# Retention attention with two FFN layers on one core: late token differences formed wide, another pair order in the opening step, splits two groups ahead

## The chip, the cores and the metric

One core of a Trainium2 chip runs the whole program. The metric is device microseconds of one execution, as the median of the runs. PE is TensorE (matmuls), DVE VectorE, ACT ScalarE, POOL GpSimd, and SP the engine from whose queue nearly all DMAs are issued. Each engine works through its own queue in order, and engines wait for each other by semaphores.

## What is computed

```python
for t in range(S):                                   # B=2, H=8, S=768, D=64
    state = gamma * state + k[:, :, t] (outer) v[:, :, t]
    y[:, :, t] = scale * q[:, :, t] @ state
x = y.transpose(0, 2, 1, 3).reshape(1536, 512)
h = x @ w_in; x = (h / (1 + exp(-h))) @ w_out        # 512 -> 2048 -> 512
h = x @ w_in; out = max(0.01 * h, h) @ w_out         # second layer, other weights
```

The state decays per head with `gamma = 1 - 2^(-5-h)`. Both layers see 1536 tokens; their weights come to the kernel as int64 words, from which float values are decoded on the chip.

## The kernel before

**Precision.** Every float operand of a large matmul is split in a rounded part h and a remainder l (`halves`: a copy on ACT, L172, and a subtraction on DVE, L173), and a product is the sum of three matmuls (`TERMS`).

**Attention.** Twelve chunks of 128 tokens, one iteration j each. In program order an iteration holds: the scaled queries of chunk j+1 (POOL, L213), the scores of j+1 (PE, L235), the scaled keys of j (POOL, L218), the decayed state (POOL, L225), the values of j (PE, L255, L264, L272), the masked scores of j+1 (DVE), `store_x(j)`, which puts the outputs of chunk j where the FFN wants them, the new state, and what the dict `behind` names for this j. From chunk 5 on the queries stand on POOL.

**Tokens.** They are kept as four sets of 384, in two pairs p, called lanes a and b. `put_first` stores the first set of a pair (`xf`, and its halves in `xa`). `put_second` forms for the second set differences `tm` on DVE (L302, L303), its halves in `xb`, and on POOL (L305, L306) two more differences in place of `xf`, chunk by chunk (128 x 256 elements each). `split_t(p, n)` makes the halves of `tm` (n = 0) and of the differences in `xf` (n = 1) into `T4[p]`, 128 x 1536 at once.

**Weights.** A weight block is loaded by two DMAs of 512 KB on SP (`load_w`, L119) into one of two staging buffers, then converted in pieces: `words` (ACT, L125 and L127), `clamp` (DVE, L131 and L135), `sign` (DVE, L142; it gives the staging buffer back, and `signed` issues the next load behind it), `low` (DVE, L149). A converted block goes to DRAM (`keep_w`, SP, L154), or is split at once (`direct`). For an up block POOL also forms four sums (`sums`, L169) into `sf`, and `split_a`, `split_s` split the blocks and the sums.

**Up projection.** Per layer eight steps; a step computes with block k a 2 x 2 arrangement of (output halves) x (sets) by seven products instead of eight. A product is 12 matmuls of 384 columns, six per lane (L357). Product 1, then 6, 7 and 4, add up in a PSUM pair X (two alternate between steps); product 2 goes to a pair Z; 5, then 3, to a pair V. After 1, 6 and 7 ACT copies X (L386) to `ct[0]`, `ct[1]`, `ct[2]`; after 2, 7 and 3 DVE adds a copy to Z or V (L390), and ACT applies the activation (L399 or L401). `keep` writes a step's result g, 1.5 MB, to DRAM (SP, L406); it stands in the step behind. `begin` writes the first step, lane by lane; `rest` each other step, in the order 6, 5, 2, 7, 1 (of the next step), 4, 3, with conversion pieces between products from `up_tasks`.

**Down projection.** 24 groups n: three token sets s of 512 and eight blocks i, 24 matmuls of 512 columns each (L434). For a group a block of g is fetched from DRAM (`fetch_g`, SP, L422) and split (`split_g`, gh). Weights of the first blocks are split before; in groups with s = 0 the remaining six are fetched from DRAM (L159) and split into `wt`. Layer 0's down projection also converts the eight up blocks of layer 1: `todo` has 32 pieces, spread over 22 groups. `finish_x` writes the end of a token set through `put_first` and `put_second` for the next layer.

**What sets the order.** All is written by hand under a manual schedule: the order in the code is the order in each engine's queue. SP's queue is shared by loads, keeps and fetches; a load that waits for `sign` holds up the fetches behind it.

Of the kernel before, what the change touches and what calls it, by code (L numbers as in the profile page):

```python
# [41 lines left out]
def retention_moe_kernel(ctx: ExitStack, tc: tile.TileContext, att, w1, w2, cst, out):  # L42
# [121 lines left out]
    def sums(w):  # L164
        A21, A22, A11, A12 = (blocks(w)[:, n] for n in range(4))
        S1, S2, S3, S4 = (sf[:, n] for n in range(4))
        for o, a, b, op in ((S1, A21, A22, ALU.add), (S3, A11, A21, ALU.subtract),
                            (S2, S1, A11, ALU.subtract), (S4, A12, S2, ALU.subtract)):
            nc.gpsimd.tensor_tensor(out=o, in0=a, in1=b, op=op)  # L169
# [118 lines left out]
    def put_first(s, a, b, ys, kept=False):  # L288
# [3 lines left out]
        for i, y in enumerate(ys):  # L292
            if not kept:
                nc.scalar.activation(out=f[:, i], in_=y, func=AF.Copy)
        for i, y in enumerate(ys):
            halves(h[:, i], l[:, i], y)

    def put_second(s, a, b, ys):
# [5 lines left out]
        halves(h, l, ys[1])  # L304
        nc.gpsimd.tensor_tensor(out=f[:, 0], in0=t[:, 1], in1=f[:, 0], op=ALU.subtract)  # L305
# [149 lines left out]
    with tc.manual_schedule():  # L455
# [32 lines left out]
        second_w = [[(l, 1, (i + 2) % Q) for i in range(Q)] for l in range(2)]  # L488
# [19 lines left out]
        def pieces(w, end=keep_w):  # L508
# [6 lines left out]
            8: lambda: (low(wa), sums(wa), split_t(0, 0)), 9: lambda: (split_a(wa), split_t(0, 1)),  # L515
            10: lambda: (split_s(wa), words(wb)),
# [27 lines left out]
        def up_tasks(layer, k):  # L544
            t = [[] for _ in range(7)]
            if layer == 0:
                if k == 0:
                    wd = first_w[3]
                    return [[lambda: split_t(1, 0)], [lambda: clamp(wb)], [lambda: signed(wb)],
                            [lambda: (low(wb), sums(wb)), lambda: split_t(1, 1)],  # L550
                            [lambda: split_a(wb)], [lambda: split_s(wb), lambda: words(wc)],
                            [lambda: clamp(wc)], [lambda: signed(wc)]]
                if k == 1:
                    wd = first_w[3]
                    return [[lambda: (low(wc), sums(wc))], [lambda: words(wd)],
                            [lambda: split_a(wc)], [lambda: split_s(wc)], [lambda: clamp(wd)],
                            [lambda: signed(wd)], [lambda: (low(wd), sums(wd))]]
                if k + 1 < Q:
                    a = first_w[k + 1]
                    t[0].append(lambda: split_a(a))  # L560
                    t[1].append(lambda: split_s(a))
# [216 lines left out]
```

## Time and profile before

| what | value |
|---|---|
| median of the runs (three) | 649.32 us (645.4 to 650.17) |
| the profiled execution's own time | 649.08 us |
| its span, first to last instruction | 647.3 us |
| PE busy | 577.3 us, 89% |
| DVE, ACT, POOL busy | 341.7, 284.9, 110.1 us |
| mean granted clock of PE | 0.944 of full speed |

A busy share counts time in which an engine executes. What an engine waits for is in the list of its waits, and a timeline row carries in brackets how long the engine was idle ahead of it and what released it. The granted clock is the share of full speed that PE had in a stretch.

### The profile page before, as it was taken

How to read it: one execution, taken by the hardware profiler on the slowest of the kernel's cores; microseconds unless marked ns; L12 is line 12 of the kernel's file. 1: busy time of each engine (PE TensorE's matmuls, PEld its weight loads, DVE VectorE, ACT ScalarE, POOL GpSimd, SP SyncE). 2: the span in 40 equal slices, each digit the busy share in tenths (PEclk: the TensorE clock that was granted, in tenths of full speed). 3: DMA queues.
4: the chain of work that ended last, by engine and by line, in shares of the span. 5: the costliest groups of instructions: out<-in, count | busy, mean ns of one | idle time of the engine just before them, and what ended most of it. 6: DMA issues, size and time to landing. Idle time of an engine off the chain costs nothing.

```text
span 647.3 us, 7975 instructions
## 1 busy us (share of the span) xinstructions
PE 577.3 (89%) x3222; PEld 510.3 (79%) x3222; DVE 341.7 (53%) x359; ACT 284.9 (44%) x337; POOL 110.1 (17%) x112
## 2 busy tenths in 40 slices
PE   9647488998888869989999979999999899999996
PEld 7546378998888857767878868999999688888885
DVE  5436364676778667546454756565665571320410
ACT  2012134666666565345324425656665470321401
POOL 3353613132333000000010242222220000000000
PEclk9768678998999979999999988999999899999999
DMA  8656001456777887664656620877773690540701
GB/s 334 256 160 231 1 2 65 164 192 230 260 261 270 287 281 267 231 229 162 218 199 184 216 89 4 274 258 244 257 271 121 224 363 31 196 129 12 249 1 65
DMA packets 35705, 121.19 MB, mean 187 GB/s; under 512 B 3282, under 2 KB 3410, under 8 KB 33620
## 3 DMA queue, kind: packets, MB, share of 16 engines
q1 hardware_dynamic: 35376, 120.34, 54.0%
q8 instruction: 25, 0.41, 0.3%
q10 hardware_dynamic: 292, 0.34, 0.2%
q14 instruction: 12, 0.10, 0.0%
HBM read 81.87 MB, written 38.80 MB: 186 GB/s over the span
## 4 chain that ended last, share of the span: by engine, by line
PE 60%; DVE 16%; DMA 8%; ACT 7%; issue 5%; POOL 3%; SPq 1%; ACTq 0%; DVEq 0%; POOLq 0%
PE p L357 27%; PE p L434 27%; DMA c<-g 4%; DVE r L142 3%; DVE r L149 3%; DVE w L173 2%; ACT w L172 2%; PE p L235 2%; PE p L255 2%; POOL sf L169 1%; PE p L264 1%; DMA sf<-g 1%; ACT c L386 1%; DMA r<-scr 1%; DVE big L390 1%
## 5 line engine op out<-in xcount | busy, mean ns | idle before, releaser
L357 PE MATMUL p<-tt,w 128*128 128x384 f32 x768 | 149.6, 346 | 18.7 <-ACT c L386 9.9
L357 PEld LDWEIGHTS p<-tt,w 128*128 128x128 f32 x768 | 138.9, 194 | 22.9 <-ACT c L386 12.2
L173 DVE TENSOR_TENSOR w<-c,w 128x1024 fp32r<-128x1024 f32 x46 | 56.6, 1230 | 122.3 <-ACT w L172 121.9
L434 PE MATMUL p<-w,wt 128*128 128x512 f32 x432 | 100.0, 391 | 4.7 <-ACT w L172 2.4
L434 PE MATMUL p<-wt,w 128*128 128x512 f32 x432 | 99.1, 390 | 1.4 <-ACT big L452 1.4
L434 PEld LDWEIGHTS p<-w,wt 128*128 128x128 f32 x432 | 80.9, 188 | 23.4 <-ACT w L172 3.6
L434 PEld LDWEIGHTS p<-wt,w 128*128 128x128 f32 x432 | 80.8, 188 | 19.1 <-ACT big L452 2.2
L172 ACT ACTIVATE w<-c 128x1024 fp32r<-128x1024 f32 x46 | 48.9, 1063 | 83.8 <-DMA c<-g 66.9
L434 PE MATMUL p<-w,w 128*128 128x512 f32 x288 | 71.8, 407 | 10.8 <-ACT w L172 7.7
L357 PE MATMUL p<-xa,w 128*128 128x384 f32 x384 | 76.9, 350 | 1.2 <-ACT c L386 1.2
L434 PEld LDWEIGHTS p<-w,w 128*128 128x128 f32 x288 | 56.3, 197 | 25.5 <-ACT w L172 9.3
L386 ACT ACTIVATE c<-p 128x768 f32<-128x768 f32 (+1 forms) x54 | 39.8, 741 | 81.1 <-PE p L357 70.3
L357 PEld LDWEIGHTS p<-xa,w 128*128 128x128 f32 x384 | 71.1, 198 | 2.5 <-ACT c L386 2.2
L390 DVE TENSOR_TENSOR big<-p,c 128x768 f32<-128x768 f32 (+1 forms) x54 | 46.7, 866 | 41.9 <-PE p L357 24.3
L169 POOL TENSOR_TENSOR sf<-r 128x256 f32<-128x256 f32 x32 | 36.6, 1164 | 173.4 <-DVE r L149 83.4
L149 DVE CUSTOM_DVE_ANT_0 r<-r,u 128x2048 uint16<-128x2048 uint16 x32 | 42.0, 1314 | 1.2
L127 ACT ACTIVATE u<-ws 128x1024 int32<-128x1024 uint32 x32 | 36.2, 1133 | 12.2 <-DVE r L149 12.2
L142 DVE SCALAR_TENSOR_TENSOR r<-ws,r 128x1024 int32<-128x1024 int32 x32 | 41.3, 1289 | 0.4
L125 ACT ACTIVATE r<-ws 128x1024 f32<-128x1024 f32 x32 | 36.3, 1135 | 9.8 <-DMA scr<-r 9.8
L305 POOL TENSOR_TENSOR big<-big 128x256 f32<-128x256 f32 (+2 forms) x9 | 8.3, 925 | 180.4 <-DMA ws<-w_dram 90.1
L173 DVE TENSOR_TENSOR w<-sf,w 128x1024 fp32r<-128x1024 f32 x18 | 22.0, 1223 | 32.2 <-ACT w L172 32.2
L357 PE MATMUL p<-xb,w 128*128 128x384 f32 x192 | 36.5, 337 | 0.7 <-DVE big L390 0.7
(74 smaller groups left out, 497.7 us busy)
## 6 DMA issues: line engine op xcount, KB each, us to landing
ws<-w_dram SPq DMA_DIRECT2D x64, 512.0 KB, 5.1
g<-big SPq DMA_DIRECT2D x16, 1536.0 KB, 6.2
c<-g SPq DMA_DIRECT2D x46, 512.0 KB, 5.5
scr<-r SPq DMA_DIRECT2D x20, 512.0 KB, 6.0
r<-scr SPq DMA_DIRECT2D x20, 512.0 KB, 7.1
att_a<-att_dram SPq DMA_DIRECT2D x18, 512.0 KB, 6.1
att_b<-att_dram SPq DMA_DIRECT2D x6, 512.0 KB, 8.4
out_dram<-big SPq DMA_DIRECT2D x11, 256.0 KB, 2.1
```

What stands on the lines that cost most here:

```text
L125: nc.scalar.activation(out=r.bitcast(F32), in_=t[:, :, :, 1].bitcast(F32), func=AF.Abs)
L127: nc.scalar.activation(out=u, in_=t[:, :, :, 0].bitcast(U32), func=AF.Copy, scale=2.0 ** -29)
L142: nc.vector.scalar_tensor_tensor(out=r, in0=t[:, :, :, 1], scalar=-0x40000000, in1=r, op0=ALU.bitwise_and, op1=ALU.bitwise_or)
L149: nc.vector.tensor_tensor(out=r, in0=r, in1=u, op=ALU.add)
L169: nc.gpsimd.tensor_tensor(out=o, in0=a, in1=b, op=op)
L172: nc.scalar.activation(out=h, in_=s, func=AF.Copy)
L173: nc.vector.tensor_tensor(out=l, in0=s, in1=h.bitcast(F32), op=ALU.subtract)
L235: nc.tensor.matmul(out=sc[:, r, c], lhsT=kT[s, c], rhs=q[s, c], start=True, stop=True)
L357: nc.tensor.matmul(out=o, lhsT=a[:, ta, k * 128:k * 128 + 128], rhs=rhs(p, tb, k), start=(begin and m == 0), stop=(end and m == 5), skip_g ...
L386: nc.scalar.activation(out=ct[n][:, c, 0:N], in_=self.X[:, c, 0:N], func=AF.Copy)
L390: nc.vector.tensor_tensor(out=self.block(f, half, lanes), in0=t[:, c, 0:N], in1=ct[n][:, c, 0:N], op=ALU.add)
L434: nc.tensor.matmul(out=y, lhsT=l, rhs=r, start=(i == 0 and f == 0 and n == 0), stop=(i == Q - 1 and f == 1 and n == 2),)
```

## The change

It is several edits of the hand-written order:

1. `put_second` no longer has the two POOL subtractions. `rest_t(p)` does them once per pair, 128 x 768 elements each: in attention at j = 10 and j = 11, behind POOL's last queries, and at layer 0's end behind `finish_x`. The sums of the first weight block are divided over j = 8, 9 and 10, its `split_s` moves to j = 11 and `split_t(0, 1)` into the opening step. `put_first` splits before it copies.
2. `begin` puts half products of the two lanes in another order: 1a 2a 1b 6a 2b 5a 7a 5b 6b 4a 3a 7b, then product 1 of the next step by lanes, 4b, 3b.
3. `rest` has the order 6, 2, 5, 7, 1, 4, 3, and the keep of the step before stands behind product 2.
4. The conversion pieces stand at other products. Steps 6 and 7 convert one weight block instead of two; down blocks 6 and 7 of layer 0 join layer 1's up blocks in `todo`, which now has 40 pieces, over 21 groups.
5. In the down projection the split of a block of g stands two groups ahead (one before), its fetch three (two before), and the first two splits stand in the last up step.

The diff, cut to its core:

```diff
-        nc.gpsimd.tensor_tensor(out=f[:, 0], in0=t[:, 1], in1=f[:, 0], op=ALU.subtract)
+    def rest_t(p):
+        f, t = xf[p], tm[p]
         nc.gpsimd.tensor_tensor(out=f[:, 0], in0=t[:, 1], in1=f[:, 0], op=ALU.subtract)
         nc.gpsimd.tensor_tensor(out=f[:, 1], in0=f[:, 1], in1=t[:, 1], op=ALU.subtract)
...
-            8: lambda: (low(wa), sums(wa), split_t(0, 0)), 9: lambda: (split_a(wa), split_t(0, 1)),
-            10: lambda: (split_s(wa), words(wb)),
+            8: lambda: (low(wa), sums(wa, (0,)), split_t(0, 0)), 9: lambda: (sums(wa, (1,)), split_a(wa)),
+            10: lambda: (sums(wa, (2, 3)), rest_t(0), words(wb)), 11: lambda: (split_s(wa), rest_t(1)),
...
-                (6, a, lambda l: s.copy(1, l)), (1, b, lambda l: s.copy(0, l)),
-                (7, a, lambda l: s.copy(2, l)), (2, b, lambda l: s.add(0, 0, 0, s.Z, l)),
+                (1, b, lambda l: s.copy(0, l)), (6, a, lambda l: s.copy(1, l)),
+                (2, b, lambda l: s.add(0, 0, 0, s.Z, l)), (5, a, lambda l: None),
...
-            seq = (6, 5, 2, 7, 1, 4, 3) if n else (6, 5, 7, 2, 4, 3)
+            seq = (6, 2, 5, 7, 1, 4, 3) if n else (6, 2, 5, 7, 0, 4, 3)
...
                     tasks[2].append(lambda: fetch_g(layer, 0, 0))
-                    tasks[5] += [lambda: split_g(layer, 0, 0), lambda: fetch_g(layer, 0, 1)]
-                    tasks[6] += [lambda: fetch_w(second_w[layer][0])]
+                    tasks[4] += [lambda: fetch_g(layer, 0, 1), lambda: split_g(layer, 0, 0)]
+                    tasks[5] += [lambda: fetch_w(second_w[layer][0])]
+                    tasks[6] += [lambda: split_g(layer, 0, 1)]
...
             steps[Q - 1].keep()
+            fetch_g(layer, 0, 2)
...
-            todo = [p for w in first_w[Q:] for p in pieces(w)] if layer == 0 else []
+            if layer == 0:
+                for w in second_w[0][6:] + first_w[Q:]:
+                    todo += pieces(w, third if w[1] else keep_w)
...
                 if n + 2 < SETS * Q:
-                    fetch_g(layer, *divmod(n + 2, Q))
-                if n + 1 < SETS * Q:
-                    split_g(layer, *divmod(n + 1, Q))
+                    split_g(layer, *divmod(n + 2, Q))
+                if n + 3 < SETS * Q:
+                    fetch_g(layer, *divmod(n + 3, Q))
...
-                    for t in todo[n * len(todo) // 22:(n + 1) * len(todo) // 22]:
+                for t in todo[n * len(todo) // 21:(n + 1) * len(todo) // 21]:
```

POOL's queue in attention, from the sums of the first weight block on: L213 are queries, L218 keys, L225 the state's decay, L169 sums (`sf`), L305 to L308 the token differences (`big`).

```order
+L169 TENSOR_TENSOR sf<-r_74 128x256
 L213 TENSOR_TENSOR att_a<-att_a,gst 128x512
 L218 TENSOR_TENSOR att_a<-att_a,cs 128x512
 L225 TENSOR_TENSOR gst<-gst,cs 128x256
-L305 TENSOR_TENSOR big<-big 128x2x128
-L306 TENSOR_TENSOR big<-big 128x2x128
+L169 TENSOR_TENSOR sf<-r_74 128x256
 L213 TENSOR_TENSOR att_b<-att_b,gst 128x512
```

The narrow pair ahead of the last queries is gone, and a single sum stands there; the pairs ahead of the queries of earlier chunks are gone with nothing in their place.

PE's queue in layer 0's fourth up step, before: six matmuls a row, two rows a product. The names after the arrow tell the product: `tt` with `w_87` is 6, 5 or 7, `xa` with `w_86` is 2, `xa` with `w_88` is product 1 of the next step; what is written is X (`p_993`), V (`p_1069`) or Z (`p_1083`).

```order
L357 MATMUL p_993<-tt_85,w_87 128x384 x6
L357 MATMUL p_993<-tt_659,w_87 128x384 x6
L357 MATMUL p_1069<-tt_85,w_87 128x384 x6
L357 MATMUL p_1069<-tt_659,w_87 128x384 x6
L357 MATMUL p_1083<-xa_64,w_86 128x384 x6
L357 MATMUL p_1083<-xa_65,w_86 128x384 x6
```

The same place in the changed kernel, where Z is `p_1059` and V `p_1079`:

```order
L359 MATMUL p_993<-tt_85,w_87 128x384 x6
L359 MATMUL p_993<-tt_649,w_87 128x384 x6
L359 MATMUL p_1059<-xa_64,w_86 128x384 x6
L359 MATMUL p_1059<-xa_65,w_86 128x384 x6
L359 MATMUL p_1079<-tt_85,w_87 128x384 x6
L359 MATMUL p_1079<-tt_649,w_87 128x384 x6
```

Product 2 and product 5 have changed places; products 7, 1, 4 and 3 follow as before.

DVE's queue at the end of layer 1's up projection, before: the weight block's `low` (L149) and split, the split of g's block 0 (`w_86<-sf`), the add of product 3 (L390), and the splits of g's block 1 (`c_69`) and of a third weight block (`wt`).

```order
L142 SCALAR_TENSOR_TENSOR r_76<-ws_73,r_76 128x1024
L149 ISA r_76<-r_76,u 128x2048
L173 TENSOR_TENSOR w_88<-r_76,w_88 128x1024
L173 TENSOR_TENSOR w_86<-sf,w_86 128x1024
L390 TENSOR_TENSOR big<-p_3322,c_70 128x2x384
L173 TENSOR_TENSOR w_89<-c_69,w_89 128x1024
L173 TENSOR_TENSOR wt_3407<-r_74,wt_3407 128x1024
```

In the changed kernel, where the split of g's block 0 is `w_651<-sf` and of block 2 `w_86<-c_70`:

```order
L142 SCALAR_TENSOR_TENSOR r_74<-ws_73,r_74 128x1024
L173 TENSOR_TENSOR w_651<-sf,w_651 128x1024
L149 ISA r_74<-r_74,u 128x2048
L173 TENSOR_TENSOR w_88<-r_74,w_88 128x1024
L173 TENSOR_TENSOR w_89<-c_69,w_89 128x1024
L392 TENSOR_TENSOR big<-p_3323,c_70 128x2x384
L173 TENSOR_TENSOR w_86<-c_70,w_86 128x1024
L173 TENSOR_TENSOR wt_3394<-r_76,wt_3394 128x1024
```

The add of product 3, on which the last keep of g depends, now also has the split of g's block 1 ahead of it.

## Rows read from the trace of the kernel before

**Rows 1.** Windows: length, busy PE, PEld, DVE, ACT, POOL; PE clock, DMA share, GB/s:
```profile
0.00:88.50 88.50, 59.66 (x726) 49.83 (x726) 41.83 (x62) 16.58 (x27) 35.69 (x44) 0.79 0.50 180
...
116.65:229.54 112.89, 103.78 (x577) 101.87 (x576) 83.65 (x85) 73.49 (x85) 28.34 (x24) 0.98 0.71 245
229.54:377.53 147.99, 135.72 (x577) 109.19 (x577) 83.44 (x83) 63.10 (x67) 8.38 (x8) 0.98 0.66 222
...
505.63:647.29 141.66, 133.38 (x577) 108.97 (x576) 38.83 (x33) 40.14 (x45) 0.00 (x0) 0.98 0.41 141
```

**Rows 2.** Waits of PE, costliest first: total us, times, longest us:
```profile
PE p L235 <- POOL att_a L213: 18.4, 3, 9.0
...
PE p L357 <- DVE big L390: 9.5, 7, 1.9
PE p L235 <- POOL att_b L213: 8.2, 2, 4.5
```

**Rows 3.** Timeline of PE in attention: start, us, ..., [idle before <-releaser]:
```profile
46.64 2.08 PE L235 MATMUL p<-att_b 64*128 64x128 f32 x16 [3.75 <-POOL att_b L213]
...
52.89 1.16 PE L235 MATMUL p<-att_a 64*128 64x128 f32 x16
...
56.65 1.16 PE L235 MATMUL p<-att_a 64*128 64x128 f32 x16
...
69.69 2.08 PE L235 MATMUL p<-att_a 64*128 64x128 f32 x16 [9.01 <-POOL att_a L213]
```

**Rows 4.** Windows, one stretch of attention:
```profile
45.00:52.00 7.00, 5.36 (x46) 4.81 (x48) 1.30 (x2) 0.00 (x0) 7.00 (x8) 0.52 0.68 252
```

**Rows 5.** Timeline of POOL in attention, around chunk 10's queries:
```profile
64.08 2.85 POOL L169 TENSOR_TENSOR sf<-r 128x256 f32<-128x256 f32 x2 [7.86 <-DVE r L149]
66.90 0.72 POOL L169 TENSOR_TENSOR sf<-sf,r 128x256 f32<-128x256 f32 x1
...
68.38 1.26 POOL L213 TENSOR_TENSOR att_a<-att_a,gst 128x512 f32<-128x512 f32 x1
```

**Rows 6.** Timeline of PE, opening of layer 0's up projection:
```profile
98.95 2.29 PE L357 MATMUL p<-tt,w 128*128 128x384 f32 x6 [0.58 <-ACT c L386]
```

**Rows 7.** Timeline of PE, then of DVE, in layer 0's up steps:
```profile
150.20 3.53 PE L357 MATMUL p<-tt,w 128*128 128x384 f32 x12 [1.92 <-DVE big L390]
...
164.33 1.64 DVE L142 SCALAR_TENSOR_TENSOR r<-ws,r 128x1024 int32<-128x1024 int32 x1
166.11 1.54 DVE L149 CUSTOM_DVE_ANT_0 r<-r,u 128x2048 uint16<-128x2048 uint16 x1
```

**Rows 8.** Timelines of PE, SP, ACT and DVE, start of layer 0's down projection:
```profile
234.80 0.79 PE L434 MATMUL p<-w,w 128*128 128x512 f32 x1 [5.26 <-ACT w L172]
...
239.85 0.33 SPq L406 DMA_DIRECT2D g<-big  x1
...
247.52 1.06 ACT L172 ACTIVATE w<-c 128x1024 fp32r<-128x1024 f32 x1 [2.60 <-DMA c<-g]
...
254.65 1.22 DVE L142 SCALAR_TENSOR_TENSOR r<-ws,r 128x1024 int32<-128x1024 int32 x1
```

**Rows 9.** Timelines of PE, DVE, SP and ACT in layer 0's down projection:
```profile
299.91 32.80 PE L434 MATMUL p<-w,wt 128*128 128x512 f32 x144
...
317.87 1.22 DVE L142 SCALAR_TENSOR_TENSOR r<-ws,r 128x1024 int32<-128x1024 int32 x1
...
322.21 1.79 SPq L422 DMA_DIRECT2D c<-g  x2
...
328.01 1.06 ACT L172 ACTIVATE w<-c 128x1024 fp32r<-128x1024 f32 x1 [6.42 <-DMA c<-g]
...
331.70 1.23 DVE L142 SCALAR_TENSOR_TENSOR r<-ws,r 128x1024 int32<-128x1024 int32 x1
```

**Rows 10.** Timelines of SP and PE, start of layer 1's down projection:
```profile
511.07 0.33 SPq L406 DMA_DIRECT2D g<-big  x1
...
521.74 8.63 PE L434 MATMUL p<-wt,w 128*128 128x512 f32 x37
```

More of the change, by code (lines that the diff above doesn't have):

```diff
@@ L162, in blocks, with sums @@
         return rs[w].bitcast(F32).rearrange("p a (b n) -> p (a b) n", b=2)
[L164 removed]
+    def sums(w, which=range(4)):
         A21, A22, A11, A12 = (blocks(w)[:, n] for n in range(4))
         S1, S2, S3, S4 = (sf[:, n] for n in range(4))
[L167 to L168 removed]
+        for o, a, b, op in [((S1, A21, A22, ALU.add), (S3, A11, A21, ALU.subtract),
+                             (S2, S1, A11, ALU.subtract), (S4, A12, S2, ALU.subtract))[n] for n in which]:
             nc.gpsimd.tensor_tensor(out=o, in0=a, in1=b, op=op)
@@ L544, in up_tasks @@
         def up_tasks(layer, k):
-            t = [[] for _ in range(7)]
-            if layer == 0:
[L547 to L557, printed above, removed]
+            t = [[] for _ in range(8)]
@@ new lines, in up_tasks @@
+            at = lambda n, *f: t[n].extend(f)
+            if layer == 0 and k < 2:
+                wd = first_w[3]
+                if k == 0:
+                    at(0, lambda: split_t(1, 0))
+                    at(1, lambda: split_t(0, 1))
+                    at(2, lambda: clamp(wb))
+                    at(3, lambda: signed(wb), lambda: split_t(1, 1))
+                    at(4, lambda: (low(wb), sums(wb)))
+                    at(5, lambda: split_a(wb), lambda: words(wc))
+                    at(6, lambda: clamp(wc))
+                    at(7, lambda: split_s(wb))
+                else:
+                    at(0, lambda: signed(wc))
+                    at(1, lambda: (low(wc), sums(wc)), lambda: words(wd))
+                    at(2, lambda: split_a(wc))
+                    at(3, lambda: split_s(wc), lambda: clamp(wd))
+                    at(5, lambda: signed(wd))
+                    at(6, lambda: (low(wd), sums(wd)))
+                return t
@@ new lines, in up_tasks @@
+                return t
+            w = second_w[1][k]
+            n, m = (first_w[Q + k + d] if k + d < Q else None for d in (1, 2))
+            if k == 0:
+                at(0, lambda: split_t(1, 0))
+                at(1, lambda: sums(n))
+                at(3, lambda: split_t(1, 1))
+                at(4, lambda: split_a(n))
+                at(5, lambda: split_s(n), lambda: fetch_w(m), lambda: words(w))
+                at(6, lambda: clamp(w))
+                at(7, lambda: signed(w), lambda: sums(m), lambda: (low(w), keep_w(w)))
+                return t
@@ L599, in up_tasks @@
+            if n:
+                at(0, lambda: split_a(n))
+                at(1, lambda: split_s(n))
+            if m:
+                at(1, lambda: fetch_w(m))
+                at(4, lambda: sums(m))
+            at(2, lambda: words(w))
+            at(3, lambda: clamp(w))
+            at(4, lambda: signed(w))
+            at(5, lambda: (low(w), direct(w) if k > 5 else keep_w(w)))
             return t
```

101 lines of the change are left out of this document (38 added, 63 removed).

## The prediction

> **What bounds the kernel now.** I read the windows by stage first, then what TensorE (PE) waited for, then the timelines of the places where it waited. The stages [rows 1]: attention 88.50 us with PE busy 59.66; the seven later steps of layer 0's up projection 112.89 with 103.78 busy; layer 0's down projection 147.99 with 135.72; down of layer 1 141.66 with 133.38. What is left of the span of 647.3, 156, are the openings of both up projections and layer 1's later steps, in which PE never waits. So PE bounds the stages, and time is to be had or lost in its waits and in its clock.
>
> The waits [rows 2]: 18.4 + 8.2 = 26.6 us of attention wait for POOL's scaled queries (L213), five waits; 9.5 us in seven waits of up to 1.9 for VectorE's (DVE) add L390, one in each later step of layer 0.
>
> Attention: a chunk's four PE groups start 3.76 us after the last chunk's when nothing hinders (52.89 to 56.65), but 6.25 when PE comes out of a wait (46.64 to 52.89): there the score matmuls take 2.08 instead of 1.16 [rows 3], at a granted clock of 0.52, so about 1.2 GHz instead of 2.4 [rows 4]. Four of the waits arise where POOL has the two narrow subtractions L305 and L306 ahead of the queries: these cannot start until DVE's tail of the chunk before is done. The 9.01 wait has another cause: four sums (2.85 for two, 0.72 and 0.72) stand ahead of L213 at 68.38, and they had to wait 7.86 for the conversion on DVE [rows 5].
>
> **Attention, -27.3.** The narrow pairs leave POOL's queue, so the four waits behind them (26.6 - 9.0 = 17.6) go. The 9.01 wait loses two or three of the four sums; one sum (beside a DVE subtraction, 1.4) and the queries (1.26) stay behind the conversion: I take 7.1 left. One wait of 0.8 for chunk 7's load comes new, an estimate: this load lands as today while the queries are asked for sooner. Idle: 26.6 - 7.1 - 0.8 = 18.7. Three chunks at about 6.25 fall to 3.76, 7.6, and the last slow chunk gives about 1. The wide subtractions (three times as many elements as a 0.72 one of [rows 5], so at most 2.2 each, an estimate) stand behind the last queries, where POOL has nothing else that PE needs. Bounds: -13 (below, second rival) and -33 (the whole 26.6 and the clock).
>
> **Opening of each layer, +1.2 twice.** PE now has half products of the two lanes next to each other in one PSUM pair: 1b then 6a, 7a then 5b, 6b then 4a, each with a copy between. A like wait of today is 0.58 behind a copy [rows 6]. Two or three more of these, less two that the order removes, plus about 0.5 for split_s(wb), which moves behind product 4b: +1.2; in layer 0 between -4 and +4, in layer 1 -3 and +3. The first copy, on which the large waits hang, has the same work ahead.
>
> **Later steps of layer 0, -11.** The wait comes about so: sign and low (1.64 and 1.54) start in DVE's queue ahead of the add of product 3 that frees the pair V, and product 5 of the next step writes V [rows 7]. The new order 6, 2, 5 puts product 2 between, which with 103.78 busy for 49 products takes 2.12 [rows 1] and so covers the wait. Seven waits of 1.9 at most, 9.5 in all, and the clock after the first (a product of 3.53 where 2.12 is usual [rows 7]), 1.5: -11. Steps 6 and 7 also convert one word instead of two. Bounds -7 (DVE and ACT at about 15.0 a step against PE's 14.7) and -12.
>
> **Layer 0's down projection, +9.5.** Its first group starts earlier: the first two splits of g are done in the up step, so n = 0 starts 2.2 after the end of up instead of 5.26 [rows 8]. But n = 2 needs the third block of g, fetched behind the keep of the last step, and this keep waits for the add of product 3, now behind the split of g1 in DVE's queue: E + 9.7 (E is the end of up) where it stood at 239.85, E + 10.3 [rows 8]. From there to the fetch's use is 7.7 [rows 8], so the early start gives nothing. Then ten words are to be converted instead of eight, over 21 groups instead of 22: a sign nearly every second group. The loop is: sign, then SP loads the next words, then, in order on SP, it issues a later fetch of g, this lands, ACT and DVE split it, and the next sign stands behind in DVE's queue. A loop of two groups took 13.83 today (sign 317.87 to sign 331.70): the fetch issued at 322.21, split from 328.01 [rows 9]. PE's price for two groups is 2 x 32.80 / 6 = 10.93 [rows 9]. Today's eight words are spread so that PE mostly covers the loop. In the changed order either the keep of the converted word no longer stands before the fetch or the clamps no longer stand behind the split: 13.83 less about one DVE operation of the sign's size (1.22), with some slack, is 12.7. Nine such loops are 114; what else DVE does between signs (splits of the third weights, each about as long as a sign, and finish_x, about 3 by my estimate) adds 6: 120. The first sign ended today 26.3 after E (254.65 + 1.22 [rows 8]); with one more split and some order ahead I take 27.9. So the last sign ends at E + 147.8, the last split before it at E + 146.5, and two groups of PE follow: 157.5 against 147.99, +9.5. Bounds: -11 when PE covers all (2.2 + 24 x 5.47, and about 4 of waits), +20 when all nine loops take 13.83.
>
> **Layer 1's down projection, +7.4.** Here E is 505.63 [rows 1]; the keep was issued at 511.07, E + 5.4, and n = 2 began at 521.74 [rows 10], E + 16.1. Now the add of product 3 stands behind low, three splits and their partners on ACT (1.06 each [rows 8], on DVE about a sign's 1.22): keep at about E + 9.4. The same keep-to-landing of 7.6 to 8.4 and two splits give n = 2 at E + 20.8: +4.7. PE idles about 7 between n = 1 and n = 2, after which I reckon 2.7 at half clock, as behind the 3.75 us wait of attention [rows 3, 4]. Who waits behind the late keep: fetches of g2 and g3 on SP, the splits on ACT and DVE, then PE. Bounds -4 (two groups begin earlier and the keep isn't late) and +9.
>
> Layer 1's later steps: 0, as PE waits for nothing there and DVE and ACT keep slack.
>
> **Sum.** -27.3 + 1.2 - 11 + 9.5 + 1.2 + 7.4 = -19.0. The profiled execution took 649.08 with a span of 647.3, 1.8 outside; its time is 0.2 under the median 649.32. 647.3 - 19.0 + 1.8 = **630**.
>
> **A rule against the row.** From its issue a fetch of g took 5.8 us to its split (322.21 to 328.01 [rows 9]), and from sign's end to the split the loop has 8.9 with a keep and a load ahead; without the keep I take 7.7. The Trainium skill, "DMA: Bandwidth & Descriptors", section "Anatomy of one DMA", gives about 2.0 us plus bytes over 436 GB/s: as an estimate 3.2 us for these 0.5 MB and 5.6 us for load and fetch together, with which the loop would fall under PE's 10.93; the sum would be about 610. The row disagrees on the 3.2, and the sum goes by the row.
>
> **Rivals.**
> 1. The fetches land sooner than I take, so the loop nearly fits. With 5.8 from issue [rows 9], nothing added for the load ahead and 0.9 for issuing this load (two fetches take 1.79 [rows 9]), the part from sign's end is 6.7 instead of 7.7; nine loops save 9 and layer 0's down comes to +0.5; in layer 1 n = 2 comes 1.5 sooner and the clock holds, +3 instead of +7.4. Time 630 - 9 - 4.4 = about **617**. For it: that row. Against: the loop of 13.83.
> 2. Attention gains only half: its loads become the bound. 88.5 us at 180 GB/s [rows 1] are 15.9 MB; in 61.2 us this needs 260 GB/s; if only 212 are had, the stage takes 75 and half the gain is gone: **644**. For it: 245 GB/s is the most that a stage here shows [rows 1]. Against: loads run ahead by four chunks.
> 3. DVE and POOL obstruct each other where the wide subtractions now stand. Two sums took 2.85 beside a DVE subtraction, and 0.72 each when alone [rows 5], so 1.4 lost. Four wide ones, each holding DVE up by 2.2, are +9: **639**. The Trainium skill, "SBUF — State Buffer", section "Who interferes with whom", says that the two engines share one port pair under an exclusive lock; the row agrees in kind.
> 4. The other side: PE falls to its lower clock in layer 0's down projection. Waits of about 1.8 then stand before nearly every second group. Today a 1.92 us wait in the up steps was followed by a product of 3.53 instead of 2.12 [rows 7]; two groups at 1.2 GHz would take 21.9, 9.2 above the loop's 12.7. Three of nine loops so are +27.6: **657.6**; from 2.1 loops on the change isn't faster. Against: the up steps kept a clock of 0.98 with seven such waits [rows 1, 2].
>
> **How the numbers follow.** Forecast 0.55 (its own range 620 to 641, from the bounds of the down loops), rivals 0.20, 0.12, 0.06, 0.07. One per cent is about what a measurement of this kernel can tell from no change: 642.8 and 655.8. Faster: 0.55 + 0.20 + 0.06 = 0.81; within: 0.12; slower: 0.07. The range runs from 608 (rival 1 with the loops wholly covered) to 645 (just past rival 2), and leaves out rival 4 and tails of the others, some 0.18.
>
> **What would show it.** Right: in attention no PE wait for L213 but one near chunk 10, and the first up product near 61; product 5 without wait in layer 0's steps; in layer 0's down projection waits of 1 to 3 us before every second group, on ACT's or DVE's splits, with a sign-to-sign distance near 12.7; in layer 1 n = 2 at 20 after up's end and one wait of about 7. Wrong: gapless down projections (rival 1), PE waiting in attention for masked scores or loads (rival 2), stretched DVE subtractions in the opening (rival 3), half clock in down (rival 4).

## The result, and the profile after

The changed kernel takes 628.64 us (median of four runs, 626.33 to 633.0) against 647.36 of the kernel before in the same comparison: a ratio of 0.972, 95% interval 0.964 to 0.979. Ratios here and below leave out executions in a slower state of the chip (one took 823.74 us), so they need not be the quotient of the medians. The forecast was 630 us, range 608 to 645. The profiled execution has a span of 628.0 against 647.3, 19.3 less; 19.0 were forecast.

Windows of the changed kernel by stage, cut at the same places as [rows 1] with the openings apart (length, then busy us of PE, its weight loads, DVE, ACT, POOL; PE's clock, DMA share, GB/s):

```profile
0.00:61.38 61.38, 50.26 (x726) 41.65 (x726) 39.68 (x61) 15.64 (x26) 32.88 (x36) 0.92 0.70 259
61.38:90.23 28.85, 22.07 (x98) 20.16 (x97) 17.82 (x20) 15.21 (x21) 7.47 (x6) 0.82 0.10 37
90.23:194.97 104.74, 101.65 (x577) 100.38 (x576) 80.13 (x82) 72.94 (x85) 27.81 (x24) 1.00 0.71 246
194.97:349.92 154.95, 140.79 (x576) 111.34 (x577) 86.87 (x86) 65.34 (x68) 10.18 (x6) 0.96 0.63 209
349.92:375.95 26.03, 20.33 (x97) 18.75 (x96) 14.69 (x17) 13.98 (x21) 11.09 (x10) 0.87 0.03 13
375.95:482.08 106.13, 102.61 (x577) 101.98 (x577) 64.15 (x66) 62.84 (x75) 18.11 (x20) 0.98 0.66 233
482.08:628.00 145.92, 134.59 (x577) 109.21 (x576) 38.01 (x32) 40.02 (x45) 0.00 (x0) 0.98 0.37 130
```

| stage | before | after | moved | forecast |
|---|---|---|---|---|
| attention | 88.50 | 61.38 | -27.1 | -27.3 |
| opening of layer 0's up projection | 28.15 | 28.85 | +0.7 | +1.2 |
| its later steps | 112.89 | 104.74 | -8.2 | -11 |
| layer 0's down projection | 147.99 | 154.95 | +7.0 | +9.5 |
| opening of layer 1's up projection | 27.32 | 26.03 | -1.3 | +1.2 |
| its later steps | 100.78 | 106.13 | +5.4 | 0 |
| layer 1's down projection | 141.66 | 145.92 | +4.3 | +7.4 |
| sum | 647.3 | 628.0 | -19.3 | -19.0 |

The total is met more closely than its terms. The signs of five terms hold; the opening of layer 1's up projection goes the other way, and its later steps, for which nothing was forecast, take 5.4 longer. What PE waits for now (total us, times, longest us), to be read against [rows 2]:

```profile
PE p L359 <- ACT c L388: 13.5, 10, 3.4
PE p L436 <- ACT wt L172: 11.0, 2, 6.0
PE p L235 <- POOL att_a L213: 6.8, 1, 6.8
PE p L436 <- DVE w L173: 5.3, 7, 0.8
PE p L359 <- DVE big L392: 4.9, 3, 3.3
```

Of the 18.4 and 8.2 us for POOL's queries in attention 6.8 and 1.2 are left. The waits for the add are gone from the later steps (the 4.9 in the last line stand in the openings). New are 11.0 us in two waits at L436: they stand before n = 2 of the two down projections.

### The profile page after: what moved, and what is told of

The parts are those of the page before. It is cut to its first block, busy times and chain, and to the rows that moved or that the text cites. A ratio compares the mean times of both kernels' runs of the same rounds, so it can differ in the third digit from the quotient of the medians.

```text
span 628.0 us, 7949 instructions
## 1 busy us (share of the span) xinstructions
PE 572.3 (91%) x3222; PEld 503.5 (80%) x3222; DVE 341.3 (54%) x359; ACT 286.0 (46%) x337; POOL 107.6 (17%) x102
## 4 chain that ended last, share of the span: by engine, by line
PE 52%; DMA 16%; DVE 14%; ACT 8%; issue 6%; POOL 3%; SPq 1%; ACTq 0%; DVEq 0%; POOLq 0%
PE p L436 25%; PE p L359 23%; DMA c<-g 9%; DMA scr<-r 3%; ACT w L172 3%; DVE w L173 2%; DVE r L142 2%; DVE r L149 2%; DVE big L392 2%; POOL sf L169 1%; DMA att_b<-att_dram 1%; DVE r L131 1%; DMA sf<-g 1%; DVE tt L173 1%; ACT u L127 1%
## 5 line engine op out<-in xcount | busy, mean ns | idle before, releaser
L436 PE MATMUL p<-w,wt 128*128 128x512 f32 x432 | 105.7, 404 | 10.8 <-ACT wt L172 5.0
L436 PEld LDWEIGHTS p<-w,wt 128*128 128x128 f32 x432 | 83.2, 194 | 33.2 <-DVE w L173 5.8
L436 PE MATMUL p<-wt,w 128*128 128x512 f32 x432 | 101.8, 397 | 7.6 <-ACT wt L172 6.0
L436 PEld LDWEIGHTS p<-wt,w 128*128 128x128 f32 x432 | 82.4, 191 | 26.6 <-ACT wt L172 6.4
L359 PE MATMUL p<-xa,w 128*128 128x384 f32 x384 | 74.4, 342 | 5.7 <-ACT c L388 5.3
L359 PEld LDWEIGHTS p<-xa,w 128*128 128x128 f32 x384 | 68.7, 192 | 6.9 <-ACT c L388 5.9
L436 PE MATMUL p<-w,w 128*128 128x512 f32 x288 | 69.2, 398 | 3.4 <-ACT w L172 1.8
L436 PEld LDWEIGHTS p<-w,w 128*128 128x128 f32 x288 | 54.9, 192 | 16.7 <-DVE w L173 2.8
L169 POOL TENSOR_TENSOR sf<-r 128x256 f32<-128x256 f32 x32 | 36.6, 1164 | 172.9 <-DVE r L149 64.9
L127 ACT ACTIVATE u<-ws 128x1024 int32<-128x1024 uint32 x32 | 36.5, 1140 | 16.2 <-DVE r L149 16.2
L149 DVE CUSTOM_DVE_ANT_0 r<-r,u 128x2048 uint16<-128x2048 uint16 x32 | 41.2, 1287 | 1.1
L125 ACT ACTIVATE r<-ws 128x1024 f32<-128x1024 f32 x32 | 36.5, 1139 | 9.3 <-DMA scr<-r 9.2
L142 DVE SCALAR_TENSOR_TENSOR r<-ws,r 128x1024 int32<-128x1024 int32 x32 | 39.6, 1237 | 0.4
L359 PEld LDWEIGHTS p<-xb,w 128*128 128x128 f32 x192 | 34.6, 192 | 0.0
```

Of the source, the lines that this page charges most:

```text
L125: nc.scalar.activation(out=r.bitcast(F32), in_=t[:, :, :, 1].bitcast(F32), func=AF.Abs)
L127: nc.scalar.activation(out=u, in_=t[:, :, :, 0].bitcast(U32), func=AF.Copy, scale=2.0 ** -29)
L142: nc.vector.scalar_tensor_tensor(out=r, in0=t[:, :, :, 1], scalar=-0x40000000, in1=r, op0=ALU.bitwise_and, op1=ALU.bitwise_or)
L149: nc.vector.tensor_tensor(out=r, in0=r, in1=u, op=ALU.add)
L359: nc.tensor.matmul(out=o, lhsT=a[:, ta, k * 128:k * 128 + 128], rhs=rhs(p, tb, k), start=(begin and m == 0), stop=(end and m == 5), skip_g ...
L436: nc.tensor.matmul(out=y, lhsT=l, rhs=r, start=(i == 0 and f == 0 and n == 0), stop=(i == Q - 1 and f == 1 and n == 2),)
```

## The experiments

Times are medians; each group of runs was made beside runs of the kernel before on the same chip, which took 649.27, 648.03 and 647.65 us. The changed kernel was timed with the first comparison alone (647.36), so a difference to its 628.64 below carries the 2 us by which these medians differ. Stage lengths are read from PE's timeline as above ("up" is an opening and its later steps together).

### The narrow subtractions back in POOL's queue

```diff
         halves(h, l, ys[1])
+        nc.gpsimd.tensor_tensor(out=f[:, 0], in0=t[:, 1], in1=f[:, 0], op=ALU.subtract)
+        nc.gpsimd.tensor_tensor(out=f[:, 1], in0=f[:, 1], in1=t[:, 1], op=ALU.subtract)

     def rest_t(p):
+        return
```

> The changed kernel with the two narrow subtractions L305 and L306 of each put_second back in POOL's queue in attention (and after layer 0), and the wide ones left out. Theory: these narrow pairs alone make four of attention's PE waits, so 4.9 + 4.5 + 3.8 + 4.5 = 17.6 us of waits come back, with 5 to 8 us of lower clock behind them; first up product near 84 instead of 61.4, time near 651. Rival: something else (DVE's tail of a chunk, or the loads) would hold the queries in any case; then under 5 us come back, time 629 to 634.

650.88 us: ratio to the kernel before 1.007, interval 1.002 to 1.012. Attention takes 85.4 instead of 61.4, 24 more. Waits of PE in this kernel:

```profile
PE p L235 <- POOL att_a L213: 16.4, 3, 6.8
...
PE p L235 <- POOL att_b L213: 8.9, 2, 5.2
```

16.4 + 8.9 less the 6.8 that the changed kernel has too are 18.5 us in four waits (17.6 were expected), and the clock of the attention falls from 0.92 to 0.80. This one edit is worth more than the whole change; the rest of it costs a few us.

### The order of products 2 and 5: taken out of the change, and put alone into the kernel before

```diff
-            seq = (6, 2, 5, 7, 1, 4, 3) if n else (6, 2, 5, 7, 0, 4, 3)
+            seq = (6, 5, 2, 7, 1, 4, 3) if n else (6, 2, 5, 7, 0, 4, 3)
```

This takes the order out of the changed kernel (except in each layer's last step, which keeps it).

> The changed kernel with products 2 and 5 of each later up step (but the last) in their old order, 6, 5, 2, 7. Theory as predicted: product 2 between covers the add of product 3, so seven waits of 1.9 before product 5 come back in layer 0, with 1.5 of lower clock: 639. Rival: the moved conversion pieces took sign and low from ahead of that add in DVE's queue, and the order alone changes nothing any more: 628 to 631, no wait before product 5.

629.77 us: no difference from the changed kernel that these runs tell. No wait before product 5 comes back. DVE and PE in its fourth later step (PE's row of 24 matmuls is products 6 and 5 in one run):

```profile
131.46 1.22 DVE L142 SCALAR_TENSOR_TENSOR r<-ws,r 128x1024 int32<-128x1024 int32 x1
132.84 1.52 DVE L149 CUSTOM_DVE_ANT_0 r<-r,u 128x2048 uint16<-128x2048 uint16 x1 [0.16 <-ACT u L127]
134.29 0.94 DVE L392 TENSOR_TENSOR big<-p,c 128x768 f32<-128x768 f32 x1
...
133.78 4.35 PE L359 MATMUL p<-tt,w 128*128 128x384 f32 x24
```

In the kernel before, sign started together with product 6 (164.33 [rows 7]; product 6 at 164.44), and the add 3.2 us after sign:

```profile
167.57 0.94 DVE L390 TENSOR_TENSOR big<-p,c 128x768 f32<-128x768 f32 x1
```

Here sign starts 2.3 us ahead of product 6, so the add comes 0.5 after product 6's start and is over before product 5 wants V. By these rows the conversion pieces that stand one product earlier do this, and not the order; no run moves them alone. For this wait the rival holds.

But the order isn't without effect. Layer 0's later steps in this run:

```profile
86.42:193.91 107.49, 102.78 (x577) 100.06 (x576) 80.32 (x82) 72.78 (x85) 27.72 (x24) 1.00 0.69 240
```

They take 107.5, where the profiles of six kernels with the new order in all these steps (the changed one among them, 104.7) have 103.5 to 104.9. Waits of 0.47, 0.39, 0.53 and 1.72, all but the 0.39 for copies, stand where the changed kernel has one of 1.48. In the length of the whole up projection, 132.9 against 133.6, this is hidden: the opening, with the same code, took 25.4 here and 28.9 there.

The reverse puts the order alone into the kernel before:

```diff
-            seq = (6, 5, 2, 7, 1, 4, 3) if n else (6, 5, 7, 2, 4, 3)
+            seq = (6, 2, 5, 7, 1, 4, 3) if n else (6, 5, 7, 2, 4, 3)
```

> The kernel before with only products 2 and 5 of each later up step (but the last) exchanged, 6, 2, 5, 7. Theory as predicted: the exchange is enough, seven waits of 1.9 go: 9.5 to 11 us less than before, near 637. Rival: the add that product 5 waits for is late by more than a product, or a wait arises elsewhere: under 4 us less, 643 to 647.

645.87 us; ratio 0.998, interval 0.994 to 1.002: no change that can be told. The waits of 1.9 do go (three of 0.35 remain), but the wait for a copy that the kernel before has at 212.51, 1.62 us, grows to 3.96. It stands in the last step that converts two weight blocks. Timelines of PE and ACT there:

```profile
205.43 4.21 PE L357 MATMUL p<-tt,w 128*128 128x384 f32 x12 [3.96 <-ACT c L386]
...
203.56 1.12 ACT L127 ACTIVATE u<-ws 128x1024 int32<-128x1024 uint32 x1 [2.30 <-DVE r L149]
204.58 1.50 ACT L386 ACTIVATE c<-p 128x768 f32<-128x768 f32 x2
```

The copy L386 that product 4 waits for stands on ACT behind L127, which writes the buffer of the low words and waits 2.30 for the first block's `low` on DVE; PE waits 3.96 and then runs a product in 4.21. So the order covers the wait, as forecast, but in the kernel before this step takes part of the gain back (22.2 instead of 18.7): up falls by 3.3 (141.0 to 137.7), where the change has 7.5 less.

### All sums behind the last queries

```diff
-            8: lambda: (low(wa), sums(wa, (0,)), split_t(0, 0)), 9: lambda: (sums(wa, (1,)), split_a(wa)),
-            10: lambda: (sums(wa, (2, 3)), rest_t(0), words(wb)), 11: lambda: (split_s(wa), rest_t(1)),
+            8: lambda: (low(wa), split_t(0, 0)), 9: lambda: split_a(wa),
+            10: lambda: (sums(wa), rest_t(0), words(wb)), 11: lambda: (split_s(wa), rest_t(1)),
```

> The changed kernel with all four sums of the first weight block behind the last queries (iteration 10) instead of one ahead of chunk 10's. Theory: the wait of 6.8 us left in attention is this one sum and the conversion ahead of it; it goes, and with it the lower clock of the chunk behind (about 3): first up product near 52, time near 619. Rival: what then stands last is the work for the first up step (sums, wide subtractions and splits on POOL, DVE and ACT), so PE waits as long in the opening: first up product near 52 but the opening longer by 5 to 10, time 626 to 629.

624.45 us. What was left of the wait in the changed kernel, on POOL and PE:

```profile
45.01 2.17 POOL L169 TENSOR_TENSOR sf<-r 128x256 f32<-128x256 f32 x1 [7.87 <-DVE r L149]
...
48.45 2.08 PE L235 MATMUL p<-att_a 64*128 64x128 f32 x16 [6.84 <-POOL att_a L213]
```

One sum of 2.17 (0.72 when alone) after low, then the queries (47.14, 1.26). Without it the wait falls to 0.46 and the lower clock behind it goes, but attention ends at 57.8, 3.6 sooner and not 10. Timeline of PE in this run:

```profile
48.83 1.09 PE L255 MATMUL p<-c,att_a 128*64 128x128 f32 x16 [1.78 <-DVE c L242]
...
54.18 1.82 PE L255 MATMUL p<-c,att_b 128*64 128x128 f32 x16 [3.23 <-DVE c L242]
```

PE now waits for masked scores (L242), which stand on DVE behind the conversion and splits. Two of these operations also take about twice as long as in the changed kernel, while POOL works beside them: the conversion's `low` 2.19 instead of 1.22 (at 43.78), a split of the weight block 2.18 instead of 0.96 (at 50.81). Neither theory's number is met: the gain is given back in part, already inside attention.

### The fetch of g's third block ahead of the last keep

```diff
-        t = sf.rearrange("p (a b) n -> p a (b n)", a=2) if n % (SETS * Q) == 0 else ct[(n % (SETS * Q) - 1) % 3]
+        t = sf.rearrange("p (a b) n -> p a (b n)", a=2) if n % (SETS * Q) == 0 else ct[(0, 2, 1)[(n % (SETS * Q) - 1) % 3]]
...
-                    tasks[6] += [lambda: split_g(layer, 0, 1)]
+                    tasks[6] += [lambda: fetch_g(layer, 0, 2), lambda: split_g(layer, 0, 1)]
...
+            fetch_g(layer, 0, 3)
             steps[Q - 1].act(0, 1)
             steps[Q - 1].keep()
-            fetch_g(layer, 0, 2)
...
-                if n + 3 < SETS * Q:
+                if n and n + 3 < SETS * Q:
                     fetch_g(layer, *divmod(n + 3, Q))
```

> The changed kernel with the third block of g fetched into the buffer that the add of product 7 frees (the copies' buffers are taken in the order 0, 2, 1), in the last up step, and the fourth block fetched ahead of the last keep instead of behind it. Theory: in both down projections the wait of 5 to 6 us before n = 2 comes from the add of product 3 and the keep ahead of that fetch on SP; it falls to 2 or less (then at n = 3), and the lower clock behind it goes: 4 to 7 us less in layer 1 (its down projection 139 to 142 instead of 146), 3 to 6 less in layer 0, whose first sign comes earlier, 617 to 622 in all. Rival: the fetch is slow in any case beside the other transfers; less than 3 in all, 626 to 629.

615.77 us, 13 less than the changed kernel and a little below the 617 to 622 expected. Start of layer 1's down projection in the changed kernel, SP and PE, to be read against [rows 10]:

```profile
489.70 0.33 SPq L408 DMA_DIRECT2D g<-big  x1
490.12 1.95 SPq L424 DMA_DIRECT2D c<-g  x2
...
499.47 1.22 PE L436 MATMUL p<-wt,w 128*128 128x512 f32 x2 [5.99 <-ACT wt L172]
```

The keep is issued 7.6 after the end of up (5.4 before the change), and n = 2 starts at 17.4 (16.1 before), after PE has waited 5.99. With the fetch ahead of the keep, PE of this run:

```profile
489.29 5.60 PE L436 MATMUL p<-wt,w 128*128 128x512 f32 x24
...
495.35 0.73 PE L436 MATMUL p<-wt,w 128*128 128x512 f32 x2 [0.46 <-ACT wt L172]
```

n = 2 follows without a wait, and 0.46 and 0.53 stand before n = 3. The window of the whole stage has 138.19 against 145.92, with the clock at 1.00 instead of 0.98:

```profile
478.21:616.40 138.19, 132.05 (x577) 107.40 (x575) 38.44 (x32) 40.38 (x45) 0.00 (x0) 1.00 0.39 136
```

Layer 0's down projection falls from 155.0 to 150.5. So the wait came from the place of this fetch, behind the late add and the keep, as forecast. The edit also puts the fourth block's fetch ahead of the keep; the two were not tried apart.

### Loads and keeps one group later

```diff
-        def signed(w):
+        def signed(w, later=False):
             sign(w)
-            load_next()
+            if later:
+                owed.append(load_next)
+            else:
+                load_next()
+
+        def ended(w, end):
+            low(w)
+            if end is keep_w:
+                owed.append(lambda: keep_w(w))
+            else:
+                end(w)
...
-            return [lambda: words(w), lambda: clamp(w), lambda: signed(w), lambda: (low(w), end(w))]
+            return [lambda: words(w), lambda: clamp(w), lambda: signed(w, True), lambda: ended(w, end)]
...
                     fetch_g(layer, *divmod(n + 3, Q))
+                while owed:
+                    owed.pop(0)()
```

> The changed kernel where in layer 0's down projection the load that follows a sign and the keep that follows a low are issued one group later, behind that group's fetch of g. Theory: the loop of 13.3 us from sign to sign is SP's queue (fetches wait for sign and low); without it PE sets the pace, signs every 11 us, and layer 0's down projection falls from 155 to 139 to 143: 613 to 617. Rival: the loop is the time of the transfers or the work of DVE and ACT; signs stay above 12.5 us apart, 624 to 629.

614.73 us, 14 less than the changed kernel. In the changed kernel a loop reads like this (DVE, SP, ACT), against [rows 9]:

```profile
286.97 1.22 DVE L142 SCALAR_TENSOR_TENSOR r<-ws,r 128x1024 int32<-128x1024 int32 x1
...
288.25 1.34 SPq L119 DMA_DIRECT2D ws<-w_dram  x2
290.16 2.02 SPq L424 DMA_DIRECT2D c<-g  x2
...
298.06 1.07 ACT L172 ACTIVATE w<-c 128x1024 fp32r<-128x1024 f32 x1 [7.37 <-DMA c<-g]
...
300.31 1.22 DVE L142 SCALAR_TENSOR_TENSOR r<-ws,r 128x1024 int32<-128x1024 int32 x1
```

Sign, load, keep, fetch at 290.16, split 7.9 later, next sign: 13.3 us for what PE does in 10.9. With loads and keeps behind the next fetch, PE of this run has no wait after the first matmuls of n = 2:

```profile
209.79 1.22 PE L436 MATMUL p<-w,wt 128*128 128x512 f32 x2 [5.04 <-ACT wt L172]
211.23 34.34 PE L436 MATMUL p<-w,wt 128*128 128x512 f32 x142 [0.22 <-DVE wt L173]
...
256.30 32.80 PE L436 MATMUL p<-w,wt 128*128 128x512 f32 x144
```

The ten signs stand 10.5 us apart in the mean (216.52 to 310.97 on DVE's timeline), in the changed kernel 13.3, and the stage takes 140.6 instead of 155.0. A fetch lands no sooner (7.9 us from its issue at the median between 216 and 312 us, in the changed kernel 7.3), but its issue no longer waits for sign and low. The loop is SP's order, and not the transfers or the work of DVE and ACT.

The same deferral in the kernel before, where the `owed` loads and keeps go behind the `fetch_g` of n + 2:

> The kernel before with the same deferral of loads and keeps behind the next fetch of g in layer 0's down projection. Theory: with eight words over 22 groups PE covered nearly all of the loop, so little is to be had: its waits behind n = 2 add to 6 us, of which 2 to 5 go; layer 0's down projection 143 to 146 instead of 148. Rival: the loop held this kernel as much as the changed one; 10 us or more go, 137 or less.

It gives 644.59 us, ratio 0.994 (0.991 to 0.997), and 143.9 instead of 148.0 in the stage. There the loop cost 4 us, in the changed kernel 14. The change adds two weight blocks to the stage, and it also sets fetches and splits a group further ahead; which of both makes the difference no run shows.

### Two smaller waits

```diff
-            seq = (6, 2, 5, 7, 1, 4, 3) if n else (6, 2, 5, 7, 0, 4, 3)
+            seq = (6, 2, 5, 7, 1, 4, 3) if n else (6, 0, 5, 7, 2, 4, 3)
...
-                if p == 7:
+                if p == (7 if n else 4):
                     s.act(0, 0)
...
-            at(2, lambda: words(w))
-            at(3, lambda: clamp(w))
-            at(4, lambda: signed(w))
-            at(5, lambda: (low(w), direct(w) if k > 5 else keep_w(w)))
+            d = 2 if k == 1 else 0
+            at(2 + d, lambda: words(w))
+            at(3 + d, lambda: clamp(w))
+            at(4 + d, lambda: signed(w))
+            at(min(5 + d, 6), lambda: (low(w), direct(w) if k > 5 else keep_w(w)))
...
-                    tasks[4] += [lambda: fetch_g(layer, 0, 1), lambda: split_g(layer, 0, 0)]
-                    tasks[5] += [lambda: fetch_w(second_w[layer][0])]
+                    tasks[4] += [lambda: split_g(layer, 0, 0)]
+                    tasks[5] += [lambda: fetch_g(layer, 0, 1), lambda: fetch_w(second_w[layer][0])]
```

With product 2 an activation and the fetch of g's second block move too.

> The changed kernel with product 2 of each layer's last up step between 7 and 4 (it stood there before the change), and in layer 1's second step the conversion pieces two products later. Theory: the two waits of 0.96 before product 4 and the wait of 2.6 with its 1.6 of lower clock in that second step go; 5 to 6 us less, 622 to 624. Rival: each comes back at another product (product 5 waits for V, a later copy waits), less than 2, 627 to 629.

627.48 us, against 628.64: no difference that these runs tell, where 5 to 6 us were expected. The two edits work against each other. The wait in layer 1's second step, in the changed kernel, ACT and PE:

```profile
385.48 1.13 ACT L125 ACTIVATE r<-ws 128x1024 f32<-128x1024 f32 x1 [3.46 <-DMA scr<-r]
...
388.28 1.50 ACT L388 ACTIVATE c<-p 128x768 f32<-128x768 f32 x2
...
389.13 3.83 PE L359 MATMUL p<-tt,w 128*128 128x384 f32 x12 [2.56 <-ACT c L388]
```

`words` (L125) waits 3.46 until the buffer of a converted block is written to DRAM, which the opening's later pieces had made late: SP issues this keep 3.0 us after the step's start at 375.95, where the kernel before issued it (404.34) 0.5 ahead of the step (404.85).

```profile
378.97 0.33 SPq L154 DMA_DIRECT2D scr<-r  x1
```

The copies behind `words` on ACT hold PE for 2.56, and a product takes 3.83. With `words` two products later this wait is gone (0.56 and 0.43 stand in the next two steps), and layer 1's up projection takes 128.7 instead of 132.2, about 1 of it by the other edit. But product 2 in the old place of the last step gives back more than its 0.96. PE at the start of layer 0's down projection in this run:

```profile
194.19 12.75 PE L436 MATMUL p<-w,w 128*128 128x512 f32 x48 [4.11 <-DVE big L392]
```

The first down matmul writes the pair that product 2 used, and waits for its add: 4.11 instead of 0.69, and 1.95 in layer 1.

### All of them, and without the exchange in the last step

> All edits of these three runs and of the run with the sums behind the last queries, in one kernel. Theory: the gains lie in different stages but for the start of layer 0's down projection, so they add to 28 to 33 us: 596 to 601. Rival: what one frees is waited for in the next stage (as the sums' 3.5 us of 10 in attention); 605 to 615.

598.38 us, as the theory has it: the gains nearly add up. Of the edits above this kernel has all but those of the first two headings. The last kernel takes the exchange of product 2 out again, with what had moved beside it:

```diff
-            seq = (6, 2, 5, 7, 1, 4, 3) if n else (6, 0, 5, 7, 2, 4, 3)
+            seq = (6, 2, 5, 7, 1, 4, 3) if n else (6, 2, 5, 7, 0, 4, 3)
```

> The kernel with all edits, but with product 2 of the last up step back where the change puts it, so that the pair Z is read out early. Theory: exchanging it made the first down matmul wait for the add of product 2 (4.1 and 1.9 us), and only hid waits of 0.96; without it 3 us less in layer 0 and 1 less in layer 1: 594 to 596. Rival: the wait has another cause; 598 or more.

593.92 us, just below the 594 to 596 expected: the first down matmul's wait of 4.1 us falls back to 0.68. The ratio to the kernel before is 0.915 (0.909 to 0.921), 35 us less than the changed kernel. Windows of this kernel: attention, up, down, up, down.

```profile
0.00:57.44 57.44, 48.82 (x727) 40.12 (x727) 41.14 (x61) 16.84 (x27) 34.61 (x36) 0.96 0.75 277
57.44:189.58 132.14, 124.23 (x674) 120.46 (x672) 98.02 (x101) 86.97 (x103) 35.27 (x30) 0.97 0.58 203
189.58:324.63 135.05, 131.92 (x576) 107.94 (x577) 85.37 (x86) 64.80 (x68) 7.73 (x6) 1.00 0.72 242
324.63:454.21 129.58, 121.84 (x674) 119.29 (x673) 80.93 (x80) 76.85 (x95) 30.95 (x30) 0.97 0.55 193
454.21:592.40 138.19, 132.05 (x577) 107.43 (x575) 38.43 (x32) 40.38 (x45) 0.00 (x0) 1.00 0.39 135
```

Both down projections now run at a clock of 1.00, with 3.1 us of waits in layer 0 and 2.4 in layer 1 (the other 3.7 there stand behind the last matmul); most of what PE still waits for lies in attention and in the openings.

## Why the prediction was right, and where it was not

**Attention: right, and by its mechanism.** 27.1 against 27.3. The wait at chunk 10 is 6.84 (7.1 taken), the new one for a load 1.2 (0.8), and with the narrow pairs back 24 us return.

**Later steps of layer 0: right in sign; the waits were miscounted, and the named cause is only a part.** The prediction has seven waits for the add, "one in each later step". Seven is the count of the whole kernel [rows 2]. Four of them stand in these steps, 7.5 us with the one of [rows 7], and three of 0.65 to 0.74 in the openings; one more wait there is for a copy. Timeline of PE in the kernel before:

```profile
168.57 2.38 PE L357 MATMUL p<-tt,w 128*128 128x384 f32 x12 [1.86 <-DVE big L390]
...
202.22 2.37 PE L357 MATMUL p<-tt,w 128*128 128x384 f32 x12 [1.86 <-DVE big L390]
...
212.51 2.37 PE L357 MATMUL p<-tt,w 128*128 128x384 f32 x12 [1.62 <-ACT c L386]
```

So the term took 9.5 where 7.5 were to be had. Measured, the waits of the stage fell from 9.1 to 3.1 and PE's busy time by 2.1 (103.78 to 101.65). The order 6, 2, 5 does cover the wait in the kernel before, but by the two runs it is worth about 3 of the 8.2 us: 3.3 put in alone, 2.7 taken out of the change. In the changed kernel the add is early without it, since pieces moved one product earlier. These moved pieces have no term in the prediction, which names only "one word instead of two", at nothing. Waits of 1.48, 0.96 and 0.64 for copies and a split are left, and the 0.96 follows from the new order itself: the last step has no product 1, so product 4 stands right behind 7, whose copy it needs.

**Layer 0's down projection: right by its mechanism, sizes within 2.5 us.** Nine loops took 119.4 (signs at 219.59 and 338.96 on DVE's timeline), 120 were reckoned; the first sign ended 25.8 after the end of up, not 27.9, for the most part since the keep came 8.2 after it and not 9.7. Waits of 0.8 to 2.0 stood before six groups behind the first sign, and not of 1 to 3 before every second. That the loop hangs on SP's order was shown by taking it away.

**Layer 1's down projection: right by its mechanism, over-sized by 3.** The keep came at 7.6 instead of 9.4 and n = 2 at 17.4 instead of 20.8 after the end of up (482.08). I had set three splits and low behind that end at full length; on DVE's timeline the first split was over by then (480.83, 1.23) and low 1.1 after it. From the keep to n = 2 were 9.8 and not 11.4. What the clock cost was met: n = 2 to 7 took 35.7 (499.47 to 535.14) against 32.6 for as many matmuls later in the stage.

**Layer 1's up projection: wrong.** "PE waits for nothing there and DVE and ACT keep slack" is the step that failed: +5.4 instead of 0. Waits of 2.56 and 0.96 came, and PE's busy time rose by 1.8 (100.78 to 102.61). The pieces of the opening had been moved back, so the keep of its block was late, and `words` of the next step waited for that buffer at the head of ACT's queue. I had followed each move to the engine that does it, but not to the buffer that it gives back. The 0.96 comes from the new order in the last step, as in layer 0.

**The openings: wrong.** Two or three more waits behind copies were forecast, +1.2 twice; they did not come. In layer 1 the waits are as long as before (5.7 and 5.8), and PE's busy time is 1.2 less at a clock of 0.87 instead of 0.81. This is no chance: the opening took 26.0 to 26.4 in nine profiled kernels with the change, 27.2 to 27.6 in three without. Why the clock is higher stays open. In layer 0 the +0.7 is luck. Of eight kernels with the same code there, four took 25.2 to 25.7 and four, the changed one among them, 27.9 to 28.9. In the long ones a wait of 3.31 for an add is followed by 12 matmuls in 3.1 to 4.2, in the short ones a wait of 1.5 to 2.4 by 12 in 2.4; what decides between them stays open.

**The rivals.** Slow loads in attention did not come: the stage moved 259 GB/s, 260 were needed. The fetches did not land sooner: 7.9 from issue where 5.8 had been seen. The Trainium skill, "DMA: Bandwidth & Descriptors", section "Anatomy of one DMA", gives its fit for a DMA that GpSimd issues; the estimate of 3.2 for the fetch alone and 5.6 with the load carried it over to DMAs that SyncE issues behind others, and these rows do not bear it out. PE's clock in layer 0's down projection was 0.96: beside the stretch behind the 5.0 us wait before n = 2 it fell twice, behind waits of 1.1 and 1.2. From 258.13 to 265.20 it was 0.76 (23 matmuls took 7.11, where 23 from 244.81 took 5.51). A fall so cost 1.6 and not the 9.2 of the fourth rival, and the loop still was the bound. That rival also counted seven waits of 1.9 in the up steps where four stand. Of the obstruction of DVE and POOL there is a trace in layer 0's opening of the changed kernel, on DVE and POOL:

```profile
63.86 1.59 DVE L173 TENSOR_TENSOR w<-sf,w 128x1024 fp32r<-128x1024 f32 x1 [0.53 <-ACT w L172]
65.38 3.39 DVE L173 TENSOR_TENSOR tt<-big,tt 128x1536 fp32r<-128x1536 f32 x1
69.15 1.74 DVE L173 TENSOR_TENSOR tt<-big,tt 128x1536 fp32r<-128x1536 f32 x1
...
62.53 1.84 POOL L307 TENSOR_TENSOR big<-big 128x768 f32<-128x768 f32 x1 [5.62 <-DVE big L302]
64.33 2.82 POOL L308 TENSOR_TENSOR big<-big 128x768 f32<-128x768 f32 x1
```

The split beside the wide subtraction takes 3.39, alone 1.74, and the subtraction 2.82 instead of 1.81. This is one loss of 1.7 and not four of 2.2. The Trainium skill, "SBUF — State Buffer", section "Who interferes with whom", gives these two engines one shared port pair under an exclusive lock. The rows agree with that: the two engines end in turn, POOL at 64.37, DVE at 65.45, POOL at 67.15, DVE at 68.77, and these ends lie 1.1, 1.7 and 1.6 apart, near what the operations take alone (1.23, 1.82 and 1.74). In the run with narrow subtractions the same split takes 1.76 and the opening 25.3 instead of 28.9; but the four short openings above have the split at 3.4 too, so it isn't what makes the long ones long, and no run shows that it costs the kernel anything.

**The total.** The errors had both signs (+2.9, -2.5, -2.5, +5.4, -3.1 for the five largest), so that the sum of 19.0 met 19.3 is luck in part: it would have been off by 3 to 4 if the opening of layer 0 had been one of the short ones.

## What to carry to other kernels

Follow a moved piece to everything that it gives back: the buffer that the next piece needs and the queue behind its DMA matter more than its own time. In an in-order DMA queue, issue the fetches whose data is ready ahead of transfers that still wait for a producer; here this brought 14 us in one place and 13 in another, where it took a changed buffer rotation to free the target in time. Moving work between stages had cost 7 and 4. Before a count of waits is spread over stages, find each of them on the timeline: seven waits in the list were four in the stage. Before a gain is put down to one of several edits, ask whether another of them would remove the same wait.

## What the runs showed of the hardware

A long wait costs a stage more than its own length, through the clock. Behind the 5.99 us wait in layer 1's down projection the granted clock was 0.54 in the first 6 us, near the lower of its two levels (1.2 of 2.4 GHz), and 1.00 from 505.50 on:

```profile
499.47:505.50 6.03, 5.81 (x14) 4.20 (x15) 5.94 (x6) 4.66 (x5) 0.00 (x0) 0.54 1.02 377
```

The six groups from there took 3 us longer than later ones, and the run that cut the waits by 5.2 us gained 7.7. The length of the wait alone does not tell whether this happens: in the kernel before, a product behind a wait of 1.92 took 3.53 [rows 7], behind waits of 1.85 and 1.86 2.35 to 2.38. When DVE and POOL obstruct each other both lengthen, the split on DVE from 1.74 to 3.39 and the subtraction on POOL from 1.81 to 2.82: they end about when they would if each waited for the other's operation to finish.
